# Reordering an expert loop: one branch for the first layer, its transposes behind the previous slot's second layer, gathers a slot sooner, the optional slots nested

## Chip, cores, metric

One core of one Trainium2 chip. The time is the device time of one execution in microseconds; several executions are taken and the median is quoted. TensorE (PE in the profile, PEld for its weight loads) does matrix products and transposes, ScalarE (ACT) and VectorE (DVE) the elementwise work, GpSimd (POOL) the gathers and scatters by index, and SyncE (SP) issues the plain transfers. Each engine runs its own instruction stream in order; streams wait for one another on semaphores. A name with a q behind it (PEldq, ACTq) is the sequencer of that engine: branches, waits, register loads.

## What is computed

A gated linear recurrence per head, then a dense layer of three maxed projections, then a mixture of eight experts in which each token goes to one expert. The change touches only the last part:

```python
logits = x @ w_gate                      # x: [3072, 384], 8 experts
e_idx = np.argmax(logits, axis=1)
gate_w = softmax(logits)[np.arange(N), e_idx]
eom = 1.0 / (1.0 + np.exp(-(x @ w_output_gate)))
for e in range(8):
    mask = e_idx == e
    h = np.maximum(x[mask] @ w1[e], 0.0)  # w1: [384, 1024]
    ye = h @ w2[e]                        # w2: [1024, 384]
    out[mask] = gate_w[mask, None] * eom[mask, e, None] * ye
```

## The kernel before

The tokens are sorted into slots of up to 128 tokens of one expert. There are 24 token tiles (NT) and so at most 32 slots (NS); how many are filled (`n_all`, from `meta`) depends on the data. Slots 0 to 2 (NF) belong to the largest expert and are begun while the routing of the last block of tokens is still computed. The loop over the other slots is unrolled, slots 24 to 31 behind a run-time condition `guard(j)`, `n_all > j`. In these inputs 30 slots are filled, 0 to 29.

A slot with at least 64 tokens, or one that is not the last of its expert, is *whole*: each of its products is three passes of rounded operands (hi times hi, hi times lo, lo times hi) with weights split beforehand by ScalarE (hi) and VectorE (lo). A last slot with fewer than 64 tokens is *alone* (`kind[j] == 1`): it is computed in plain fp32 straight from the staged weights, the two halves of the weights side by side. Which it is, is known at run time only, so each step holds both forms in an If/Else (`by_kind`).

The steps of slot j, in the names of the code:

- `gather(j)`: POOL fetches the slot's rows of x (384 values and the token's weight) into `xg[j]`, four buffers.
- `tx(j)`: 3 transposes of `xg` on PE into `psT`, then ACT (hi, L812, or plain, L816) and DVE (lo, L813).
- `cast1(j)`, `split2(j)`: if the expert is new (`new[j]`), 6 copies and 6 subtractions for the first layer's weights, 8 and 8 for the second's (L625, L626). Each layer has one buffer of split weights and two of staged ones (`stage`, SP, 1.5 MB each).
- `up(j, h)`: first layer, half h: 9 products of 512 columns (L844) and a copy to `hs` by ACT (L845). Alone: all of it in the call with h = 1 (L833, L853).
- `th(j)`: 8 transposes of `hs` (L884; alone 4, L889), then ACT's relu and DVE's remainder into `ch` (L863, L864; alone L890).
- `down(j)`: second layer, 24 products of 384 columns (L903; alone L833), then ACT scales with the token's weight (L917, `yo`; alone also L921 and L922) and POOL scatters to the output (L923).

The order on the engines is the order in which the code is written (a manual schedule). For slot j the loop writes: kinds of slot j+3 loaded into registers; 2 pieces of `split2(j)`; `gather(j+3)`; `up(j+1, 0)`; `th(j)`; the other 6 pieces of `split2(j)`; `up(j+1, 1)`; `tx(j+2)`; the first layer's weights of j+3 staged; `cast1(j+2)`; `down(j)`; the second layer's weights of j+2 staged.

Where a branch is not taken, the engines whose work it skips must still bring their semaphores to the count that the other way would have left. A form with work in both ways does that on its own instructions; a way that is empty on an engine gets an event instruction that waits until the engine has finished all it was given before, and then adds the count. `up(j+1, 0)` is such a case: written with `If(kind == 0)` and no Else.

Of the kernel before, what the change touches and what calls it, by code (L numbers as in the profile page):

```python
# [33 lines left out]
NS = NT + NE  # L34
# [54 lines left out]
def _layers(ctx, tc, pool_, wk, K, general, qk, al, a0, v, vT, w123, wout, gates, ew1, ew2, out):  # L89
# [508 lines left out]
    xg, cx, cxF, hs, ch, chg, new, eos, kind = ({} for _ in range(9))  # L598
# [105 lines left out]
    def slots_a_ops():  # L704
        ci = rtmp["ci"] = wt([128, NE], "ci", I32)
        nc.vector.scalar_tensor_tensor(ci, rtmp["ps"][:, 64:64 + NE], 127.0, gap, op0=ALU.add, op1=ALU.add)
        yield
        cj = wt([128, NE], "cj", I32)
        nc.vector.tensor_single_scalar(cj, ci, 7, op=ALU.arith_shift_right)
        yield  # L710
        nsl = wt([128, NE], "nsl")
        nc.vector.tensor_copy(nsl, cj)
        yield
        nf = wt([128, NE], "nf")
        nc.vector.tensor_mul(nf, nsl, nfirst)
        yield
        nc.vector.tensor_reduce(isf, nf, op=ALU.add, axis=AX.X)
        yield
        nc.vector.tensor_sub(nsl, nsl, nf)
        yield  # L720
        end = rtmp["end"] = wt([128, NE], "end")
        nc.vector.tensor_tensor_scan(end, one8, nsl, isf, ALU.mult, ALU.add)
        yield
        base = rtmp["base"] = wt([128, NE], "base")
        nc.vector.tensor_sub(base, end, nsl)
        yield
        bf = wt([128, NE], "bf")
        nc.vector.tensor_mul(bf, base, nfirst)
        yield
        nc.vector.tensor_sub(base, base, bf)  # L730
        yield
# [29 lines left out]
    def slots_e():  # L761

        end = rtmp["end"]
        rem = wt([128, NE], "rem", I32)
# [31 lines left out]

    def gather(j):
        xg[j] = C["cr"].tile([128, XW], F32, tag="xg", name="xg", bufs=4)
        n = TF * 128 if j < NF else NTOK
        nc.gpsimd.indirect_dma_start(out=xg[j], out_offset=None, in_=x2d[:n, :],  # L800
                                     in_offset=bass.IndirectOffsetOnAxis(ap=gidx[:, j:j + 1], axis=0),
                                     bounds_check=n - 1, oob_is_err=False)

    def tx(j):
        ps = bank(C["psT"], "T", "psT")
        for k in range(3):
            nc.tensor.transpose(ps[:, k * 128:(k + 1) * 128], xg[j][:, k * 128:(k + 1) * 128], ident)
        cx[j] = bp.tile([128, 2, DM], F32R, tag=("xH", "xL")[j % 2], name="cx")
        cxF[j] = bp.tile([128, DM], F32, tag="hH", name="cxF", bufs=7)
# [25 lines left out]
    def up(j, h):  # L835
        w1H, w1L = C["w1"]
        fs = slice(h * 512, h * 512 + 512)

        def whole():
            ps = bank(psM, "M", "psM1")  # L840
            for k in range(3):
                ks = slice(k * 128, (k + 1) * 128)
                for n, (x, w) in enumerate(((0, w1H), (0, w1L), (1, w1H))):
                    mm(ps, cx[j][:, x, ks], w[:, k, fs], start=(k + n == 0), stop=(k + n == 4))  # L844
            nc.scalar.copy(hs[j][:, fs], ps)  # L845

        def alone():
            ps = bank(psM, "M", "psM1")
            w = C["s1"][j % 2]
            for k in range(3):  # L850
                x = cxF[j][:, k * 128:k * 128 + 64]
                halves(ps, 512, (x, x), [w[:, k, g * 512:(g + 1) * 512] for g in range(2)], k == 0, k == 2)
            nc.scalar.copy(hs[j][:, :512], ps)  # L853

        if h == 0:
            hs[j] = bp.tile([128, FF2], F32, tag="x32", name="hs")
            with tc.If(kind[j] == 0) if j in kind else nullcontext():
                whole()
        else:
            by_kind(j, whole, alone)  # L860
# [14 lines left out]
    def th(j):  # L875
        ch[j] = bp.tile([128, 2, FF2], F32R, tag=f"o{j % 2}", name="ch", bufs=1)
# [17 lines left out]
    def down(j, fs=(0, NE)):  # L894
# [21 lines left out]
        gate = xg[j][:, DM:XW]  # L916
        nc.scalar.activation(y, ps[:, :DM], AF.Copy, scale=gate)  # L917
        if j in kind:
            with tc.If(kind[j] > 0):  # L919
                t = bp.tile([128, DM], F32, tag="hL", name="ylo", bufs=7)  # L920
                nc.scalar.copy(t[:64], ps[64:, :DM])  # L921
                nc.vector.scalar_tensor_tensor(y[:64], t[:64], gate[:64], y[:64], op0=ALU.mult, op1=ALU.add)  # L922
# [4 lines left out]
    def every():  # L927
        with tc.For_i(0, NTOK, 128) as r:
# [8 lines left out]
            for e in range(NE):  # L937
# [4 lines left out]
                for h in range(2):  # L942
                    up(0, h)
# [203 lines left out]
    then(up, 0, 0)  # L1147
    then(route_a, i)
    then(up, 0, 1)
    then(route_b, i)  # L1150
    then(th_whole, 0, 0)
    then(up, 1, 0)
# [4 lines left out]
    then(up, 1, 1)  # L1157
# [5 lines left out]
    then(up, 2, 0)  # L1163
    then(up, 2, 1)
# [35 lines left out]
    def guard(j):  # L1200
        return tc.If(n_all > j) if j >= NT else nullcontext()

# [10 lines left out]
    up(NF, 0)  # L1213
    up(NF, 1)
    tx(NF + 1)
    cast1(NF + 1)
    down(2)
    for j in range(NF, NS):
        if j + 3 < NS:
            load_meta(j + 3)  # L1220
            load_kind(j + 3)
        with tc.If(new[j] > 0):
            split2(j, range(2))
        if j + 3 < NS:
            gather(j + 3)
        with guard(j):  # L1226
            if j + 1 < NS:
                with guard(j + 1):
                    up(j + 1, 0)
            th(j)  # L1230
        with tc.If(new[j] > 0):
            split2(j, range(2, NE))
        if j + 1 < NS:
            with guard(j + 1):
                up(j + 1, 1)
                if j + 2 < NS:
                    tx(j + 2)
        if j + 3 < NS:
            stage(j + 3, ((0, "s1"),))
        if j + 2 < NS:  # L1240
            cast1(j + 2)
        with guard(j):  # L1242
            down(j)
        if j + 2 < NS:
            stage(j + 2, ((1, "s2"),))
# [50 lines left out]
```

## Time and profile before

| | us |
|---|---|
| median of 3 runs (754.25 to 758.59) | 754.65 |
| the profiled execution, its own time | 753.41 |
| its span, first to last instruction | 751.7 |
| PE busy in the span | 707.7 |
| DVE, ACT, POOL busy | 378.6, 305.8, 109.3 |

The span is what the profile shows; 1.7 us lie around it. The first filled slots begin at about 470 us, the loop over slots 3 to 29 at 494 us, and the last product ends at 740.7 us.

### The profile page before, as it was taken

What the parts mean: (1) busy time and instruction counts of PE and PEld (TensorE: products, weight loads), DVE (VectorE), ACT (ScalarE), POOL (GpSimd) and SP (SyncE); (2) the same over time, 40 slices, a digit from 0 to 9 for tenths busy, and PEclk for the clock granted to TensorE, in tenths of its full rate; (3) what the DMA queues carried; (4) which work ended last, traced back from release to release, by engine and by line L of the source; (5) the groups of instructions that cost most, each with busy time, mean ns of one, the idle gap of its engine ahead of it and who ended that gap; (6) DMA issues with size and microseconds to landing.
All of it is one profiled execution on the core that took longest, in us unless ns stands there. A gap on an engine that the chain in (4) does not pass through costs nothing. (4 is left out here: it accounts for less than half of the span.)

```text
span 751.7 us, 14582 instructions
## 1 busy us (share of the span) xinstructions
PE 707.7 (94%) x4750; PEld 627.8 (84%) x4750; DVE 378.6 (50%) x806; ACT 305.8 (41%) x750; POOL 109.3 (15%) x118
## 2 busy tenths in 40 slices
PE   7789999999999999999999999999999999999893
PEld 7668999888899998999999988899966789974663
DVE  7977887476976647546233366411115341111432
ACT  4355443554444434434222234333327453333552
POOL 1000000011120111111111130222222222222221
PEclk9999999999999999999999999999999999999997
DMA  9815400651510413100000050111387711179750
GB/s 259 349 39 157 145 1 22 183 135 28 143 40 22 129 44 106 38 22 10 16 24 13 21 200 33 49 39 44 128 303 285 280 45 44 54 263 392 284 211 17
DMA packets 23807, 86.78 MB, mean 115 GB/s; under 512 B 8004, under 2 KB 11868, under 8 KB 19600
## 3 DMA queue, kind: packets, MB, share of 16 engines
q1 hardware_dynamic: 18576, 73.54, 29.1%
q0 software_dynamic: 3968, 11.03, 4.5%
q10 hardware_dynamic: 1152, 0.89, 0.5%
q8 instruction: 51, 0.84, 0.5%
q14 instruction: 60, 0.49, 0.2%
HBM read 131.43 MB, written 10.63 MB: 189 GB/s over the span
## 5 line engine op out<-in xcount | busy, mean ns | idle before, releaser
L440 PE MATMUL hps<-xH,wH 128*128 128x384 f32 x432 | 104.0, 348 | 0.9 <-ACT xH L352 0.8
L903 PE MATMUL psP<-w2H,ch 128*128 128x384 f32 x368 | 101.4, 346 | 2.2 <-ACT ch L863 1.4
L466 POOL TENSOR_TENSOR hL<-hm,hH 128x384 fp32r<-128x384 f32 x36 | 42.2, 1172 | 399.9 <-ACT hH L461 399.8
L440 PE MATMUL hps<-xH,wL 128*128 128x384 f32 x432 | 98.4, 335 | 1.7 <-DVE wL L409 1.7
L440 PE MATMUL hps<-xL,wH 128*128 128x384 f32 x432 | 98.5, 335 | 0.0
L844 PE MATMUL psM<-w1H,cx 128*128 128x512 f32 x276 | 96.2, 404 | 0.8 <-ACTq L1204 0.8
L864 DVE SCALAR_TENSOR_TENSOR ch<-psH,ch 128x512 fp32r<-128x512 f32 x46 | 29.7, 686 | 106.1 <-ACT ch L863 105.8
L440 PEld LDWEIGHTS hps<-xH,wH 128*128 128x128 f32 x432 | 74.1, 188 | 6.9 <-ACT xH L352 1.5
L440 PEld LDWEIGHTS hps<-xH,wL 128*128 128x128 f32 x432 | 76.9, 188 | 2.3 <-DVE wL L409 2.3
L440 PEld LDWEIGHTS hps<-xL,wH 128*128 128x128 f32 x432 | 77.3, 188 | 0.2 <-DVE xL L353 0.2
L903 PEld LDWEIGHTS psP<-w2H,ch 128*128 128x128 f32 x368 | 68.1, 191 | 3.2 <-ACT ch L863 1.6
L476 PE MATMUL ops<-wo,hH 128*128 128x400 f32 x258 | 68.4, 346 | 0.4 <-ACT hH L461 0.3
L844 PEld LDWEIGHTS psM<-w1H,cx 128*128 128x128 f32 x276 | 51.9, 188 | 14.6 <-issue 1.8
L903 PE MATMUL psP<-w2L,ch 128*128 128x384 f32 x184 | 62.5, 340 | 0.0
L447 DVE TENSOR_TENSOR hm<-hm,hps 128x384 f32<-128x384 f32 x48 | 26.5, 551 | 69.6 <-PE hps L440 62.4
L923 POOL DMA_INDIRECT out<-yo,sidx x30 | 30.6, 1019 | 196.1 <-ACTq L919 132.9
L461 ACT CAST hH<-hm 128x384 fp32r<-128x384 f32 x43 | 22.0, 513 | 80.2 <-DVE hm L450 76.3
L844 PE MATMUL psM<-w1L,cx 128*128 128x512 f32 x138 | 54.5, 395 | 0.0
L917 ACT ACTIVATE yo<-psP,xg 128x384 f32<-128x384 f32 x30 | 17.4, 581 | 83.3 <-PE psP L903 64.1
L845 ACT COPY hs<-psM 128x512 f32<-128x512 f32 x46 | 27.0, 588 | 52.7 <-PE psM L844 48.2
L476 PEld LDWEIGHTS ops<-wo,hH 128*128 128x128 f32 x258 | 46.9, 188 | 1.5 <-ACT hH L461 0.7
L476 PE MATMUL ops<-wo,hL 128*128 128x400 f32 x129 | 44.4, 344 | 0.5 <-POOL hL L466 0.5
(215 smaller groups left out, 1145.7 us busy)
## 6 DMA issues: line engine op xcount, KB each, us to landing
s1a<-in_ew SPq DMA_DIRECT2D x15, 1536.0 KB
s2a<-in_ew SPq DMA_DIRECT2D x15, 1536.0 KB
s1b<-in_ew SPq DMA_DIRECT2D x15, 1536.0 KB
s2b<-in_ew SPq DMA_DIRECT2D x15, 1536.0 KB
ws<-in_w SPq DMA_DIRECT2D x6, 1152.0 KB
at<-in_al SPq DMA_DIRECT2D x16, 336.9 KB
vt<-in_v SPq DMA_DIRECT2D x8, 576.0 KB
x2d<-xs SPq DMA_DIRECT2D x24, 192.0 KB
```

The costliest lines, as they stand in the source:

```text
L440: mm(ps, slab(a, f)[:, w, k], b[i][:, k], start=(n == 0), stop=(n == 8))
L447: nc.vector.tensor_max(m, m, ps)
L461: nc.scalar.copy(hH[i, f], m)
L466: (nc.gpsimd if not general and i > 1 else nc.vector).tensor_sub(hL[i, f], hps["m"], hH[i, f].bitcast(F32))
L476: mm(ps[:, :DM + NG], a[i, f][:, ts_], wo[f // 3][:, b, f % 3], start=(f + n == 0), stop=(f + n == 7))
L844: mm(ps, cx[j][:, x, ks], w[:, k, fs], start=(k + n == 0), stop=(k + n == 4))
L845: nc.scalar.copy(hs[j][:, fs], ps)
L864: nc.vector.scalar_tensor_tensor(lo, ps, 0.0, hi.bitcast(F32), op0=ALU.max, op1=ALU.subtract)
L903: mm(ps[:, :DM], ch[j][:, x, f * 128:(f + 1) * 128], w[:, f], start=(f + n == 0), stop=(f == NE - 1 and n == 2))
L917: nc.scalar.activation(y, ps[:, :DM], AF.Copy, scale=gate)
L923: nc.gpsimd.indirect_dma_start(out=out[:, :], out_offset=bass.IndirectOffsetOnAxis(ap=sidx[:, j:j + 1], axis=0), in_=y, in_offset=None, bo ...
```

## The change

`up` loses its second call: one `by_kind` holds both halves (whole) or the alone form. `th(j+1)` is written behind `down(j)`. `tx` copies the token weight of `xg` into a small tile of its own (`gate`), so that `xg[j]` is free after `tx(j)` and no longer after `down(j)`, and `gather` runs four slots ahead in place of three. `split2(j)` is written in one piece. From slot 24 on each slot's work stands inside the condition of the one before it, and tiles made there are taken from an earlier slot (`held`). Some small tiles of the routing share a buffer under another name (left out below).

```diff
+    def held(tiles, j, n, make):
+        return tiles[j - n] if j >= NT + n else make()
+
     def gather(j):
-        xg[j] = C["cr"].tile([128, XW], F32, tag="xg", name="xg", bufs=4)
+        xg[j] = held(xg, j, 4, lambda: C["cr"].tile([128, XW], F32, tag="xg", name="xg", bufs=4))
...
     def tx(j):
+        gate[j] = held(gate, j, 4, lambda: wk.tile([128, 1], F32, tag="gate", name="gate", bufs=4))
+        nc.vector.tensor_copy(gate[j], xg[j][:, DM:XW])
         ps = bank(C["psT"], "T", "psT")
...
-    def up(j, h):
+    def up(j, hs_=(0, 1)):
         w1H, w1L = C["w1"]
-        fs = slice(h * 512, h * 512 + 512)
+        if hs_[0] == 0:
+            hs[j] = held(hs, j, 2, lambda: bp.tile([128, FF2], F32, tag="x32", name="hs"))
 
         def whole():
-            ps = bank(psM, "M", "psM1")
-            for k in range(3):
-                ks = slice(k * 128, (k + 1) * 128)
-                for n, (x, w) in enumerate(((0, w1H), (0, w1L), (1, w1H))):
-                    mm(ps, cx[j][:, x, ks], w[:, k, fs], start=(k + n == 0), stop=(k + n == 4))
-            nc.scalar.copy(hs[j][:, fs], ps)
+            for h in hs_:
+                fs = slice(h * 512, h * 512 + 512)
+                ps = bank(psM, "M", "psM1")
+                for k in range(3):
+                    ks = slice(k * 128, (k + 1) * 128)
+                    for n, (x, w) in enumerate(((0, w1H), (0, w1L), (1, w1H))):
+                        mm(ps, cx[j][:, x, ks], w[:, k, fs], start=(k + n == 0), stop=(k + n == 4))
+                nc.scalar.copy(hs[j][:, fs], ps)
...
-        if h == 0:
-            hs[j] = bp.tile([128, FF2], F32, tag="x32", name="hs")
-            with tc.If(kind[j] == 0) if j in kind else nullcontext():
-                whole()
-        else:
-            by_kind(j, whole, alone)
+        by_kind(j, whole, alone)
...
-        gate = xg[j][:, DM:XW]
-        nc.scalar.activation(y, ps[:, :DM], AF.Copy, scale=gate)
+        nc.scalar.activation(y, ps[:, :DM], AF.Copy, scale=gate[j])
...
-    up(NF, 0)
-    up(NF, 1)
+    up(NF)
     tx(NF + 1)
     cast1(NF + 1)
+    gather(NF + 3)
     down(2)
-    for j in range(NF, NS):
+    th(NF)
...
+    def turn(j):
         if j + 3 < NS:
             load_meta(j + 3)
             load_kind(j + 3)
+        if j + 4 < NS:
+            gather(j + 4)
         with tc.If(new[j] > 0):
-            split2(j, range(2))
-        if j + 3 < NS:
-            gather(j + 3)
-        with guard(j):
-            if j + 1 < NS:
-                with guard(j + 1):
-                    up(j + 1, 0)
-            th(j)
-        with tc.If(new[j] > 0):
-            split2(j, range(2, NE))
+            split2(j)
         if j + 1 < NS:
             with guard(j + 1):
-                up(j + 1, 1)
+                up(j + 1)
                 if j + 2 < NS:
                     tx(j + 2)
-        if j + 3 < NS:
-            stage(j + 3, ((0, "s1"),))
-        if j + 2 < NS:
-            cast1(j + 2)
-        with guard(j):
-            down(j)
-        if j + 2 < NS:
-            stage(j + 2, ((1, "s2"),))
+                    if j + 3 < NS:
+                        stage(j + 3, ((0, "s1"),))
+                    cast1(j + 2)
+        down(j)
+        if j + 1 < NS:
+            with guard(j + 1):
+                if j + 2 < NS:
+                    stage(j + 2, ((1, "s2"),))
+                th(j + 1)
+                if j + 1 >= NT:
+                    turn(j + 1)
+
+    for j in range(NF, NT):
+        turn(j)
```

## Rows read from the trace of the kernel before

**Rows 1.** Busy time by stretch: stretch, its length, busy us of each engine (instructions), TensorE clock, DMA.

```profile
552.00:608.00 56.00, 54.41 (x292) 38.12 (x293) 21.80 (x39) 30.59 (x63) 14.69 (x14) 1.00 0.74 266
608.00:670.00 62.00, 62.00 (x346) 56.39 (x343) 13.34 (x24) 20.80 (x41) 12.26 (x12) 1.00 0.27 86
670.00:741.00 71.00, 63.50 (x333) 43.05 (x331) 24.75 (x44) 34.65 (x70) 15.42 (x15) 0.98 0.71 264
```

**Rows 2.** Transposes of `hs`, 470 to 741 us, grouped (busy, mean ns | idle before <-releasers); PE's timeline.

```profile
L884 PE MATMUL psH<-ident,hs 128*128 128x128 f32 x160 | 20.9, 273 | 3.2 <-ACTq L919 1.5 <-PEq L857 1.1 <-PEq L1228 0.6
...
L889 PE MATMUL psH<-ident,hs 128*128 128x128 f32 x28 | 4.3, 275 | 2.3 <-ACT yo L917 0.9 <-ACTq L919 0.8 <-PEq L857 0.6
```

```profile
561.23 0.41 PE L889 MATMUL psH<-ident,hs 128*128 128x128 f32 x2 [0.59 <-PEq L857]
...
586.56 0.41 PE L884 MATMUL psH<-ident,hs 128*128 128x128 f32 x2 [0.56 <-PEq L857]
...
680.06 0.41 PE L889 MATMUL psH<-ident,hs 128*128 128x128 f32 x2 [0.84 <-ACTq L919]
```

**Rows 3.** Line 857 in the whole span: sequencer's duration ns min/median/max, first and last start.

```profile
L857 PEldq COMPARE_BRANCH  x50: 66/172/326, 481.8 to 722.5; - x50
...
L857 PEldq EVENT_SEMAPHORE  x7: 51/51/51, 551.5 to 714.3; - x7
```

**Rows 4.** ACT's timeline around 561 us.

```profile
560.67 0.58 ACT L917 ACTIVATE yo<-psP,xg 128x384 f32<-128x384 f32 x1 [3.64 <-PE psP L903]
```

**Rows 5.** PE's timeline, transposes of x and the second layer behind them, two slots.

```profile
581.57 0.41 PE L903 MATMUL psP<-w2H,ch 128*128 128x384 f32 x1 [0.30 <-PE psT L807]
...
708.88 0.52 PE L807 MATMUL psT<-ident,xg 128*128 128x128 f32 x3 [1.55 <-DMA xg<-x2d,gidx]
709.83 0.41 PE L903 MATMUL psP<-w2H,ch 128*128 128x384 f32 x1 [0.43 <-PE psT L807]
```

**Rows 6.** PE's timeline: the second layer of an alone slot.

```profile
564.99 2.80 PE L833 MATMUL psP<-s2a,hs 128*64 128x384 f32 x16
```

**Rows 7.** POOL's timeline, 698 to 701 us, and the gathers' time to landing, whole span.

```profile
698.39 1.00 POOL L923 DMA_INDIRECT out<-yo,sidx  x1 [6.73 <-ACT hs L845]
699.70 1.04 POOL L800 DMA_INDIRECT xg<-x2d,gidx  x1 [0.30 <-ACT hs L845]
```

```profile
DMA to landing us min/median/max: 3.0/4.0/9.1
```

**Rows 8.** Line 884 in one undisturbed slot, 502 to 506 us: first and last start.

```profile
L884 PE MATMUL psH<-ident,hs x6: 270/272/273, 505.4 to 506.0; 128*128 128x128 f32 x6
L884 PEldq EVENT_SEMAPHORE  x1: 51/51/51, 502.3 to 502.3; - x1
```

**Rows 9.** Line 787, registers for the kinds, on PE's sequencer.

```profile
L787 PEldq TENSOR_LOAD <-kinds x29: 297/302/483, 478.4 to 720.8; - x29
```

**Rows 10.** Line 685, a VectorE instruction of one element a partition.

```profile
L685 DVE TENSOR_SCALAR lack<-fm x1: 143/143/143, 435.1 to 435.1; 128x1 f32<-128x1 f32 x1
```

**Rows 11.** Slot 29, the last: timeline of PE, then of DVE.

```profile
731.86 1.06 PE L884 MATMUL psH<-ident,hs 128*128 128x128 f32 x8 [0.58 <-PEq L1228]
734.28 0.44 PE L903 MATMUL psP<-w2H,ch 128*128 128x384 f32 x1 [1.36 <-ACT ch L863]
...
735.01 0.98 PE L903 MATMUL psP<-w2H,ch 128*128 128x384 f32 x2
```

```profile
733.12 1.03 DVE L626 TENSOR_TENSOR w2L<-s2b,w2H 128x384 fp32r<-128x384 f32 x2
734.26 1.29 DVE L864 SCALAR_TENSOR_TENSOR ch<-psH,ch 128x512 fp32r<-128x512 f32 x2
```

**Rows 12.** Sequencers at the end: lines 1242, 80 and 1292.

```profile
L1242 POOLq INC_SWDGE_SEM  x2: 1382/1397/1412, 742.0 to 743.8; - x2
```

```profile
L80 PEldq COMPARE_BRANCH  x1: 4422/4422/4422, 742.7 to 742.7; - x1
```

```profile
L1292 POOLq DRAIN  x1: 5200/5200/5200, 745.7 to 745.7; - x1
```

More of the change, by code (lines that the diff above doesn't have):

```diff
@@ L597, in _layers @@
     C = {}
-    xg, cx, cxF, hs, ch, chg, new, eos, kind = ({} for _ in range(9))
+    xg, cx, cxF, hs, ch, chg, new, eos, kind, gate = ({} for _ in range(10))
     def open_right():
@@ L713, in slots_a_ops @@
         yield
-        nf = wt([128, NE], "nf")
+        nf = wt([128, NE], "fc")
         nc.vector.tensor_mul(nf, nsl, nfirst)
@@ L726, in slots_a_ops @@
         yield
-        bf = wt([128, NE], "bf")
+        bf = wt([128, NE], "fv")
         nc.vector.tensor_mul(bf, base, nfirst)
@@ L763, in slots_e @@
         end = rtmp["end"]
-        rem = wt([128, NE], "rem", I32)
+        rem = wt([128, NE], "cj", I32)
         nc.vector.tensor_single_scalar(rem, rtmp["ci"], 127, op=ALU.bitwise_and)
@@ L807, in tx @@
             nc.tensor.transpose(ps[:, k * 128:(k + 1) * 128], xg[j][:, k * 128:(k + 1) * 128], ident)
-        cx[j] = bp.tile([128, 2, DM], F32R, tag=("xH", "xL")[j % 2], name="cx")
-        cxF[j] = bp.tile([128, DM], F32, tag="hH", name="cxF", bufs=7)
+        cx[j] = held(cx, j, 2, lambda: bp.tile([128, 2, DM], F32R, tag=("xH", "xL")[j % 2], name="cx"))
+        cxF[j] = held(cxF, j, 2, lambda: bp.tile([128, DM], F32, tag="hH", name="cxF", bufs=7))
         def parts(hi, lo, p):
@@ L875, in th @@
     def th(j):
-        ch[j] = bp.tile([128, 2, FF2], F32R, tag=f"o{j % 2}", name="ch", bufs=1)
+        ch[j] = held(ch, j, 2, lambda: bp.tile([128, 2, FF2], F32R, tag=f"o{j % 2}", name="ch", bufs=1))
         p0 = bank(C["psH"], "H", "psH")
@@ L921, in down @@
                 nc.scalar.copy(t[:64], ps[64:, :DM])
-                nc.vector.scalar_tensor_tensor(y[:64], t[:64], gate[:64], y[:64], op0=ALU.mult, op1=ALU.add)
+                nc.vector.scalar_tensor_tensor(y[:64], t[:64], gate[j][:64], y[:64], op0=ALU.mult, op1=ALU.add)
         nc.gpsimd.indirect_dma_start(out=out[:, :], out_offset=bass.IndirectOffsetOnAxis(ap=sidx[:, j:j + 1], axis=0),
@@ L941, in every @@
                 split2(0)
-                for h in range(2):
-                    up(0, h)
+                up(0)
                 for h in range(2):
@@ L1146, in _layers @@
     i = NBLK - 1
-    then(up, 0, 0)
+    then(up, 0, (0,))
     then(route_a, i)
-    then(up, 0, 1)
+    then(up, 0, (1,))
     then(route_b, i)
     then(th_whole, 0, 0)
-    then(up, 1, 0)
+    then(up, 1, (0,))
     then(lambda: run(slots_a_ops(), route_c_ops(i), route_d_ops(i)))
@@ L1156, in _layers @@
     then(tx, 2)
-    then(up, 1, 1)
+    then(up, 1, (1,))
     then(slots_b)
@@ L1162, in _layers @@
     then(split_first, 2, NE - 1)
-    then(up, 2, 0)
-    then(up, 2, 1)
+    then(up, 2, (0,))
+    then(up, 2, (1,))
     then(slots_c)
@@ L1198, in _layers @@
         load_kind(j)
-    def guard(j):
-        return tc.If(n_all > j) if j >= NT else nullcontext()
     def cast1(j):
@@ L1212, in _layers, with guard @@
     cast1(NF)
-    up(NF, 0)
-    up(NF, 1)
+    up(NF)
     tx(NF + 1)
     cast1(NF + 1)
+    gather(NF + 3)
     down(2)
-    for j in range(NF, NS):
+    th(NF)
+    def guard(j):
+        return tc.If(n_all > j) if j >= NT else nullcontext()
+    def turn(j):
         if j + 3 < NS:
```

## The prediction

> **What bounds the kernel now.** I read the page first, for the shares: PE is busy for 707.7 of 751.7 us, so time can only be won where PE stands still, or by giving it less to do, and this change gives it the same products and transposes in another order. So the second view is the busy time by stretch, cut where the filled slots change their character [rows 1]. Between 608 and 670 us, where whole slots follow one another, PE is busy for 62.00 of 62.00 us: nothing to win there. Between 552 and 608 us 1.59 us are missing, between 670 and 741 us 7.50 us. In these two stretches lie the alone slots (10, 11, 14, 23, 24, 25, 28). DMA's share is 0.74 and 0.71 there against 0.27, since each of them needs weights of its own.
>
> The third view is the idle time ahead of the transposes of `hs`, first grouped, then one by one [rows 2]. The groups give 3.2 + 2.3 = 5.5 us in eight places; 0.58 us of it belong to the last slot [rows 11], and 4.9 us to seven places of 0.56 to 0.89 us, of which three rows stand. These are the transposes of the slots 9, 10, 13, 22, 23, 24 and 27, each the one before an alone slot; between two whole slots none are late. Twice the second layer begins late behind the transposes of x, by 0.30 and 0.43 us, and once these transposes wait 1.55 us for a gather [rows 5]: 2.28 us. The last slot has 0.58 and 1.36 us [rows 11]. Together 4.9 + 2.28 + 1.94 = 9.1 us, what is missing in the two stretches.
>
> **What causes the seven holes.** The view names several releasers for them, ACT's output step among them, and that has to be settled, because the answer decides on the sign of the change. In the old code the next slot's `up(j+1, 0)` is written ahead of these transposes, and for an alone slot its branch is empty on PE. The line's own rows show an event on PE's sequencer exactly seven times, from 551.5 to 714.3 us [rows 3], as many as there are alone slots, each at the end of the second layer before it. Such an event waits until PE is empty; behind it a branch (0.17 us [rows 3]), a wait and the first weight load have to run with nothing queued. The rival cause is ACT's output step `yo`, which ends at about the same time. But at 561.23 us PE starts while `yo` runs until 560.67 + 0.58 = 561.25 us [rows 4]: here at least it isn't waited for. I take the emptied queue as the cause of all seven; from slot 23 on, as at 680.06 us, a guard comes on top (0.84 against 0.56 and 0.59 us [rows 2]).
>
> **The change, part by part.**
>
> *One branch for the first layer.* Neither form is empty on PE any more, so the seven events go: −4.9 us at most. What is late next? `th(j+1)` now stands behind `down(j)` and needs ACT's copy of `hs(j+1)`. ACT makes it right behind `split2(j)`, which `down(j)` itself needs, and `down(j)` then runs for 2.8 us even where it is alone [rows 6]; so the copy is there. In return ACT's relu of `th(j+1)` has all of `up(j+2)` to end in, in place of one half. Nothing new is late on PE, and I take the full 4.9 us. The reordering itself costs nothing: the same 53 PE instructions of a whole slot, with one changeover fewer.
>
> *The path of the sequencer.* Between `th(j+1)` and `up(j+2)` PE's sequencer now loads the next kind (0.30 us [rows 9]) and passes some three branches of 0.17 us [rows 3], about 1.05 us with the checks. Before, this stood behind `down`. Is there work in the queue to hide it? The wait ahead of the transposes of one slot is passed at 502.3 us, and these start at 505.4 us [rows 8]: the sequencer is 3.1 us ahead. So 1.05 us are hidden. If only the eight transposes covered it (0.9 us, as they start 0.11 us apart [rows 8]), 0.15 us would show in each of 26 slots, 4 us. I take 0 and keep 4 as a bound. [...]
>
> *Gathers a slot sooner.* The gather of slot 28 is issued at 699.70 us, right behind the scatter that POOL takes first [rows 7], and lands just before its transposes start at 708.88 us, about 9 us later. The slowest of the run took 9.1 us, the median 4.0 us [rows 7]. The two late second layers (0.30, 0.43 us) are of the same origin: where PE's sequencer is held at a gather until just before the transposes, it isn't ahead any longer, and the branches behind them show. In the new order the gather keeps its place behind the scatter of slot j−1 but is the one of slot j+4: it gets one more slot, at least two stretches of 2.8 us [rows 6], one for each layer. −2.28 us. On POOL it is the same number of instructions. Its buffer is free since `tx(j)`, two slots back, so it waits for nothing new, and nor does the scatter behind it.
>
> *The copy of the weight.* One VectorE instruction of one element a partition per slot, 0.14 us by the nearest row [rows 10], 30 times, on a VectorE that is busy for 13.34 of 62 us where whole slots follow one another [rows 1]; it waits for the gather as PE's transposes do, and VectorE's next step waits for these anyhow. 0 us.
>
> *`split2` in one piece.* For a new expert's slot its first two pieces now come behind ACT's relu instead of ahead of it. Where `up(j+1)` lies between, that is covered. The last slot has no `up` behind it. In the old order two pieces precede the relu, and PE's products start at 734.28, and in earnest at 735.01 us, with VectorE's remainder for `ch` [rows 11]. In the new order the relu comes about 0.9 us sooner, but the second product needs VectorE's first w2L, behind 1.29 us for `ch`: 734.26 − 0.9 + 1.29 + 0.5 = 735.15 us [rows 11]. From there on both run at the same pace; the clock, 1.00 elsewhere and 0.98 over the last stretch [rows 1], I leave as it was. I put the last slot at +0.1 us, between −0.6 (its hole of 0.58 us counts after all) and +0.6 (one more piece is waited for).
>
> *Nesting.* Filled slots from 24 on pass two guards where there were four; hidden as above. Behind the last slot, POOL passes the empty slots 30 and 31: two count instructions of 1.4 us and branches, then 5.2 us until it is empty [rows 12], which is the end of the program. Nested, the two counts stay, since two scatters are skipped, some branches go, and six levels have to be left. I take 0, between −1.5 (one count for both) and +2.
>
> *Staging.* Its order on SP is the old one; the alone slots come up to 0.9 us sooner, and their weights are issued a full slot or more ahead. 0 us.
>
> **The sum.** 4.9 + 2.28 − 0.1 = 7.1 us. On the profiled execution: 753.41 − 7.1 = 746.3 us. The median of the runs stands 1.24 us above that execution, so 747.5 us, 0.95% less. A measurement of this kernel tells about 1% from no change, so this forecast lies on the line.
>
> **Rivals.**
>
> *A. The sequencer shows* (0.15): 4 us come back at the start of `up`, 751.5 us. For it: the holes of 0.30 and 0.43 us are of that kind [rows 5]. Against it: the 3.1 us [rows 8].
>
> *B. Transposes wait for `yo`* (0.07), the slower side: if the transposes do need ACT's output step, then, as they stand right behind `down(j)` in every slot now, 27 slots pay 4.9 / 7 = 0.7 us each, 18.9 us, less the 7.1 us won: 766.5 us. From 7.1 / 0.7 = 10 slots on the change loses. For it: the groups put 3.2 of 5.5 us down to ACT [rows 2]. Against it: the overlap at 561.23 us [rows 2, 4].
>
> *C. The gather isn't sooner* (0.08): it stays behind the scatter on POOL, and if its buffer comes free late, only 4.8 us are won: 749.8 us. Against it: the buffer's last reader moves ahead by two steps.
>
> *D. The end shrinks too* (0.12): one count instruction and the branches go, 1.4 us or more, 746.1 us or less.
>
> *E. A far jump* (0.06): the skip over slots 30 and 31 is one long jump now. The longest jump of the program, over the code of line 80, holds PE's sequencer for 4.42 us [rows 12], against 0.17 us for a usual branch; on POOL it would add some 3 to 4 us to the end: 751 us. [...]
>
> **How the numbers follow.** The forecast has 0.52, by itself 746 to 749 us. The range, 745.0 to 752.5 us, takes in A, C, E and most of D; B is left out. Faster by over 1% (below 747.1 us): a good third of the forecast's own, and D, 0.33. Slower by over 1%: B and a little, 0.08. Within 1%: 0.59.
>
> **What the new profile would show.** Right: no event of PE's sequencer in `up`; the first transposes of the slots before the alone ones without idle time; those of slot 28 without a wait for DMA; PE full from 552 to about 733 us but for the last slot. Wrong: idle time of PE ahead of `th` with ACT as its releaser in whole slots (B), or ahead of `up` with PE's sequencer (A); a longer stretch from the last scatter to the end (E).

## The result, and the profile after

The changed kernel takes 748.40 us in the median of 22 runs (742.36 to 754.86), the kernel before 755.71 us in as many runs beside it (749.95 to 759.73): a ratio of 0.9898, 95% interval 0.9874 to 0.9922. Forecast were 747.5 us and a range of 745.0 to 752.5 us. The profiled execution took 750.23 us with a span of 748.4 us, only 3.3 us less than the one of before; so the first thing to settle is where these two traces part.

They part long before the change. Busy time by stretch of the kernel after, and behind it the same ten microseconds of the kernel before (columns as in [rows 1]):

```profile
40.00:50.00 10.00, 8.93 (x63) 7.61 (x64) 5.61 (x11) 5.38 (x16) 0.00 (x0) 0.50 0.01 2
```

```profile
40.00:50.00 10.00, 8.33 (x90) 6.81 (x91) 7.43 (x13) 6.31 (x18) 0.00 (x0) 1.00 0.02 5
```

In this execution TensorE's granted clock was 0.83 from 30 to 40 us, 0.50 from 40 to 50 us and 0.65 from 50 to 60 us, in work that the change doesn't touch, where the kernel before has 1.00 in all three; and all that follows stands about 5.6 us later: the first transposes of x behind slot 2's first layer begin at 487.07 us, not at 481.44. (In two kernels of the experiments below, whose clock from 30 to 60 us was 0.66 and 1.00, they begin at 488.03 and 481.70 us.) In both kernels the long executions are mostly those with the lower mean clock (in the changed one 0.976 at 754.86 us, 0.996 at 742.36 us; in the one before, beside the experiments, 0.976 at 760.83 us, 0.995 at 750.22 us); where in an execution the clock falls, only the one profiled shows. I therefore compare from there on. Call S the stretch from these transposes (slot 3's) to the end of the last work that isn't slot 29's second layer. First the kernel before, then after, over S:

```profile
481.44:732.92 251.48, 242.89 (x1320) 194.17 (x1320) 66.20 (x114) 103.77 (x205) 55.61 (x54) 1.00 0.50 179
```

```profile
487.07:730.82 243.75, 241.46 (x1320) 194.67 (x1320) 69.91 (x141) 104.12 (x203) 55.47 (x54) 1.00 0.51 184
```

The same 1320 PE instructions take 7.73 us less: PE's idle time falls from 8.59 to 2.29 us, its busy time by 1.43 us. The last slot's second layer with its waits takes 8.23 us against 7.75, the end behind the last product 9.39 against 11.03. So −7.73 + 0.48 − 1.64 = −8.89 us, and with the 5.63 us of the early clock −3.3 us, the difference of the spans. In this one pair of executions the change is worth −8.89 us. The medians of many runs say −7.3 us, the ratio about −7.7; why less, no run shows.

Where is the idle time left? The stretches that answer to [rows 1], 5.6 us later, and PE's groups from 486 to 741 us (as in [rows 2]):

```profile
557.60:613.60 56.00, 56.00 (x306) 40.56 (x305) 25.52 (x51) 32.77 (x67) 14.49 (x14) 1.00 0.74 271
613.60:675.60 62.00, 62.00 (x346) 55.21 (x346) 12.55 (x25) 21.01 (x39) 13.75 (x14) 1.00 0.29 96
675.60:730.80 55.20, 53.68 (x293) 35.85 (x289) 18.97 (x39) 28.13 (x56) 11.88 (x12) 1.00 0.86 321
```

```profile
L907 PE MATMUL psP<-w2H,ch 128*128 128x384 f32 x345 | 94.6, 345 | 1.7 <-ACT w2H L625 1.7
L853 PE MATMUL psM<-w1H,cx 128*128 128x512 f32 x240 | 80.6, 404 | 2.0 <-ACT w1H L625 1.3 <-ACTq L1203 0.8
L907 PE MATMUL psP<-w2L,ch 128*128 128x384 f32 x173 | 58.9, 340 | 0.5 <-DVE w2L L626 0.5
...
L888 PE MATMUL psH<-ident,hs 128*128 128x128 f32 x160 | 21.0, 274 | 0.0
...
L893 PE MATMUL psH<-ident,hs 128*128 128x128 f32 x28 | 4.4, 278 | 0.0
```

Ahead of the transposes of `hs` (L888, L893) PE now stands idle for 0.0 us, where [rows 2] have 3.2 and 2.3; the stretch around slots 9 to 14 is full. Of the group L853, 0.8 us are the wait at slot 3, which both kernels have; the 1.3 us behind ACT's `w1H` are new. The timelines of PE, then of ACT, then of SP show where they come from:

```profile
694.11 0.66 PE L893 MATMUL psH<-ident,hs 128*128 128x128 f32 x4
696.02 0.49 PE L853 MATMUL psM<-w1H,cx 128*128 128x512 f32 x1 [1.25 <-ACT w1H L625]
696.74 0.50 PE L853 MATMUL psM<-w1L,cx 128*128 128x512 f32 x1 [0.23 <-DVE w1L L626]
```

```profile
695.35 3.23 ACT L625 CAST w1H<-s1a 128x512 fp32r<-128x512 f32 x6 [3.37 <-DMA s1a<-in_ew]
```

```profile
681.32 0.33 SPq L794 DMA_DIRECT2D s2a<-in_ew  x1
684.51 0.33 SPq L794 DMA_DIRECT2D s1a<-in_ew  x1
687.73 0.33 SPq L794 DMA_DIRECT2D s2b<-in_ew  x1
```

Slot 26 opens a new expert. Its first layer waits 1.48 us for the cast weights, ACT for the transfer: issued at 684.51 us, used from 695.35 us, nearly 11 us. The DMA engines (last columns: share and GB/s) are full all that time (1.01), behind a stretch in which they were not (0.61):

```profile
664.00:676.00 12.00, 12.00 (x67) 9.41 (x65) 2.73 (x5) 4.31 (x8) 3.92 (x4) 1.00 0.61 208
676.00:700.00 24.00, 22.48 (x120) 13.08 (x117) 5.63 (x12) 10.34 (x20) 4.25 (x5) 1.00 1.01 402
```

At the end, slot 29 in PE's timeline, and the sequencers of PE and POOL at line 1240, to be set beside [rows 11, 12]:

```profile
729.73 1.09 PE L888 MATMUL psH<-ident,hs 128*128 128x128 f32 x8
732.56 0.44 PE L907 MATMUL psP<-w2H,ch 128*128 128x384 f32 x1 [1.74 <-ACT w2H L625]
733.47 0.69 PE L907 MATMUL psP<-w2L,ch 128*128 128x384 f32 x1 [0.46 <-DVE w2L L626]
```

```profile
L1240 PEldq COMPARE_BRANCH  x2: 184/850/1517, 737.0 to 739.2; - x2
...
L1240 POOLq COMPARE_BRANCH  x2: 38/44/50, 739.8 to 741.5; - x2
...
L1240 POOLq INC_SWDGE_SEM  x1: 1427/1427/1427, 740.0 to 740.0; - x1
```

The last slot's waits are 2.20 us, against 0.58 + 1.36 + 0.11 = 2.05 us before. POOL counts once (INC_SWDGE_SEM), not twice.

### The profile page after: what moved, and what is told of

Same layout as the page of the kernel before. It is cut to its first block, busy times and chain, and to the rows that moved or that the text cites. A ratio compares the mean times of both kernels' runs of the same rounds, so it can differ in the third digit from the quotient of the medians.

```text
span 748.4 us, 14138 instructions
## 1 busy us (share of the span) xinstructions
PE 714.6 (95%) x4750; PEld 635.8 (85%) x4750; DVE 381.7 (51%) x837; ACT 306.8 (41%) x750; POOL 109.8 (15%) x118
## 3 DMA queue, kind: packets, MB, share of 16 engines
q0 software_dynamic: 3968, 11.03, 4.5%
## 5 line engine op out<-in xcount | busy, mean ns | idle before, releaser
L853 PE MATMUL psM<-w1H,cx 128*128 128x512 f32 x276 | 92.9, 404 | 2.0 <-ACT w1H L625 1.3
L853 PEld LDWEIGHTS psM<-w1H,cx 128*128 128x128 f32 x276 | 52.0, 188 | 13.9 <-ACT w1H L625 1.5
L853 PE MATMUL psM<-w1L,cx 128*128 128x512 f32 x138 | 54.7, 396 | 0.2 <-DVE w1L L626 0.2
L920 ACT ACTIVATE yo<-psP,gate 128x384 f32<-128x384 f32 x30 | 17.4, 581 | 82.9 <-PE psP L907 67.9
```

What stands on the lines that cost most here:

```text
L920: nc.scalar.activation(y, ps[:, :DM], AF.Copy, scale=gate[j])
```

## The experiments

Each ratio is to the kernel before, run beside it, with medians of 753.57 to 756.11 us; so ratios compare across rows better than medians do. S, PE's idle time in it and the end (from the last product to the end of the span) are those of one profiled execution each. Three more kernels, which leave part of the weights out, stand behind the table; two of them have one execution.

| kernel | S, us | idle in S | of it gathers / holes at the empty branch / slot 26 | end, us | median, us (95% interval of the ratio) |
|---|---|---|---|---|---|
| before | 251.48 | 8.59 | 2.28 / 4.96 / 0 | 11.03 | 755.71 (1) |
| after | 243.75 | 2.29 | 0 / 0 / 1.48 | 9.39 | 748.40 (0.9874 to 0.9922) |
| before, gathers sooner | 248.55 | 6.09 | 0 / 4.75 / 0 | 11.00 | 752.56 (0.9956 to 1.0023) |
| before, one branch | 249.17 | 5.96 | 5.20 / 0 / 0 | 11.04 | 750.76 (0.9917 to 0.9983) |
| after, two branches | 245.25 | 3.85 | 0 / 3.05 / 0 | 9.39 | 746.84 (0.9868 to 0.9945) |
| after, gathers later | 248.78 | 5.32 | 4.56 / 0 / 0 | 9.88 | 751.39 (0.9924 to 0.9999) |
| after, not nested | 244.70 | 2.97 | 0 / 0 / 1.47 | 11.01 | 749.56 (0.9896 to 0.9960) |
| after, second weights later | 267.45 | 16.72 | 0 / 0 / 0 | 9.39 | 773.13 (1.0184 to 1.0274) |
| after, four pieces early | 243.86 | 2.01 | 0 / 0 / 1.00 | 9.60 | 746.97 (0.9864 to 0.9949) |
| after, three buffers | 241.63 | 0.77 | 0 / 0 / 0 | 9.39 | 743.84 (0.9829 to 0.9922) |

**The gathers alone.**

```diff
...
-        if j + 3 < NS:
-            gather(j + 3)
+        if j + 4 < NS:
+            gather(j + 4)
```

> The kernel before, with nothing but the gather of slot j+4 in place of slot j+3 and the copy of the weight column that this needs. Measured by the stretch from the first transpose of slot 3's x to the end of the last product, which no early stretch disturbs: 259.2 us in the kernel before, 252.0 us in the changed one. My theory: the 2.28 us of late gathers (1.55 us ahead of the transposes of x, 0.43 and 0.30 us ahead of two second layers) go, the seven holes ahead of the transposes of hs stay: 257.0 us, and the time behind the last product stays at 11.0 us. The device time falls by 2.3 us, 0.3%. Rival C (the gather isn't sooner): 259.2 us.

The edit has the copy of the token weight too (left out above). The gather waits are gone and the holes at the branch are there, as PE's groups show:

```profile
L887 PE MATMUL psH<-ident,hs 128*128 128x128 f32 x160 | 20.9, 273 | 3.2 <-ACTq L921 1.4 <-PEq L1231 0.6 <-PEq L860 0.6
L810 PE MATMUL psT<-ident,xg 128*128 128x128 f32 x84 | 14.1, 277 | 0.8 <-issue 0.8
```

To the last product it is 256.25 us where 257.0 was expected; over S −2.93 us, of which 2.50 are idle time. Rival C falls: the gather is sooner. The device time moves less than its interval.

**One branch alone.**

```diff
-            if j + 1 < NS:
-                with guard(j + 1):
-                    up(j + 1, 0)
             th(j)
...
-                up(j + 1, 1)
+                up(j + 1)
```

> The kernel before, with nothing but the first layer of slot j+1 in one branch, behind the transposes of slot j's hs, so that these stand behind the second layer of slot j-1 in every slot. Gathers, the guards and the two pieces of split2 are the old ones. Theory of the empty branch: the seven holes (4.9 us) go and the late gathers (2.28 us) stay, while slot 26 may wait up to 1.5 us for its first layer's weights, as it does in the changed kernel: the stretch from slot 3's transposes of x to the last product falls from 259.2 to between 254.3 and 255.8 us. Rival B (the transposes wait for ACT's output step): 0.7 us of idle time ahead of them in each of 27 slots, 259.2 - 4.9 + 18.9 = 273 us.

Half right. No hole is left ahead of the transposes of `hs` (27 slots have them right behind a second layer here, and rival B's 0.7 us is in none), but to the last product it is 257.33 us, above the expected range: the gathers' waits grew from 2.28 to 5.20 us.

```profile
L882 PE MATMUL psH<-ident,hs 128*128 128x128 f32 x160 | 20.9, 274 | 0.0
L807 PE MATMUL psT<-ident,xg 128*128 128x128 f32 x84 | 14.1, 277 | 4.9 <-DMA xg<-x2d,gidx 4.0 <-issue 0.9
```

The holes had hidden these waits. The gather whose transposes stand at 571.08 us here is issued at the old time (560.34 us; S begins 6.59 us later, so 553.75 on the old clock, against 553.68). But PE comes to these transposes 1.5 us sooner, and the gather takes 10.6 us to land in place of 8.7; before, it was 2.1 us in time.

**Two branches at the new place.** The undo of the same part:

```diff
-            for h in hs_:
+            for h in (hs_[:1] if j in kind else hs_):
...
+        if j in kind:
+            with tc.If(kind[j] == 0):
+                whole()
+            hs_ = (1,)
         by_kind(j, whole, alone)
```

> The changed kernel, with the first layer of slot j in two branches again (the first half if the slot is whole; then the second half or the whole of the alone form), both at the new place. Theory of the empty branch: seven events of PE's sequencer are back in the line of the first layer, at the same slots, each with a hole of 0.56 to 0.89 us, which now stands ahead of the alone form's first products instead of ahead of the transposes of hs, since the place of the empty branch makes it, not the work behind it. The three holes of the slots 23 to 25 may be paid by the 1.5 us that slot 26 waits for its weights, which then go: the stretch of 252.0 us becomes 255.4 to 256.9 us. Rival: the holes came from where the transposes of hs stood (ACT's output step, or its copy of hs): no holes, 252.0 us.

The seven events are back, now in line 865, the new first condition; and the holes stand ahead of the alone form's first products:

```profile
L865 PEldq EVENT_SEMAPHORE  x7: 51/51/51, 552.8 to 710.2; - x7
```

```profile
553.18 1.08 PE L839 MATMUL psM<-s1a,cxF 128*64 128x512 f32 x4 [0.42 <-PEq L865]
```

Six of 0.42 and one of 0.53 us, 3.05 us in all; slot 26 no longer waits; S is 1.50 us longer, as 3.05 − 1.48 says. So the cause stands, and the hole goes where the empty branch goes, but its size was expected too high (0.56 to 0.89). To the last product it is 252.18 us, below the expected 255.4 to 256.9, for two reasons: the holes are smaller, and the last slot's second layer, with a granted clock of 1.00 in the ten microseconds around it and not 0.83, took 6.93 us, not 8.23. That stretch is no measure for a difference of 1 us; S is a better one. By the device time, one can't tell this kernel from the changed one (ratios 0.9906 and 0.9898).

**The gathers later again.**

```diff
-        if j + 4 < NS:
-            gather(j + 4)
+        if j + 3 < NS:
+            gather(j + 3)
```

> The changed kernel, with the gathers of slot j+3 again, all else as it is. Theory: a gather that is issued a slot later lands just before its transposes or behind them, as in the kernel before: about 2.3 us of idle time ahead of the transposes of x of slot 28 and of two second layers; the stretch of 252.0 us becomes 254.3 us. If only the wait of slot 28 counts: 253.5 us. Rival: the new order alone makes the old distance enough, since the gather now stands ahead of the whole first layer: 252.0 us.

More than expected: 4.56 us of waits in seven places, two of them for slot 28:

```profile
707.11 0.52 PE L813 MATMUL psT<-ident,xg 128*128 128x128 f32 x3 [1.73 <-DMA xg<-x2d,gidx]
708.17 0.66 PE L907 MATMUL psP<-w2H,ch 128*128 128x384 f32 x1 [0.55 <-PE psT L813]
```

S is 5.03 us longer: +4.56, −1.48 as slot 26's weights are in time again, and 2 us of busy time at a clock of 0.96 behind 690 us. The rival falls. Of the 4.56 us, 2.67 stand where the kernel before has its 2.28 (ahead of slot 28 and of an earlier second layer); the other 1.89 us, in two slots where it has none, are there because PE, without the holes, comes sooner.

**Not nested.** Each guard for itself, `with guard(j)` around `down(j)` and so on; the order stays. Staging and casts (`stage`, `cast1`) stand outside the guards again, as before.

> The changed kernel, with the guards of the slots from 24 on side by side as they were before, not nested; order, gathers and the one branch stay. Theory: the nesting is what shortened the end: the two skipped scatters of the slots 30 and 31 are counted twice again, and the time from the last product to the end of the program goes from 9.35 back to 11.0 us, while the stretch from slot 3 to the last product stays at 252.0 us within 0.3 us: device time +1.7 us. Rival 1: the end is shorter because the last transfers of weights no longer stand behind the last slot, or by chance: 9.35 us stays. Rival 2: the two extra guards of each slot from 24 on are seen on PE as well: the stretch grows by 0.2 us or more in each of six slots, 253 us.

The end is 11.01 us again, with two counts of 1.4 us:

```profile
L1239 POOLq INC_SWDGE_SEM  x2: 1392/1402/1412, 735.5 to 737.3; - x2
```

So the nesting gives the 1.6 us, most of it by the count of 1.4 us. Rival 1 isn't tested apart: the edit also brings back a staging issue of SP behind the last slot (0.07 us at 734.30 us). The second count, on POOL's way to the end, accounts for the time without it. S is 0.95 us longer, more than the 0.3 expected, but not by guards: 0.57 us are a wait of slot 24's second layer for its weights and 0.16 us a wait for a cast; 0.27 us are busy time. A kernel without this edit (the next one) has the first of them too, 0.54 us.

**A transfer cut, the wrong one.**

```diff
-            nc.sync.dma_start(out=C[s][j % 2], in_=...
+            m = 1 if (n, j) == (1, 26) else (3, NE)[n]
+            nc.sync.dma_start(out=C[s][j % 2][:, :m], in_=...[:, :m],
```

> The changed kernel, but of the second layer's weights of slot 26 only an eighth is loaded (the rest of that tile keeps the weights of slot 24, so the outputs of this slot's expert are others). In the changed kernel the weights for slot 26's first layer are issued at 684.5 us, and ACT can begin with them at 695.4 us; PE waits 1.25 + 0.23 us. The second layer's weights, issued 3.2 us later, are not needed before 706 us. Theory (the transfers share the DMA engines, and a later one slows an earlier one): without 1.4 MB at 0.41 MB per us the first layer's weights are there up to 3.4 us sooner, the 1.48 us go, and the stretch of 252.0 us becomes 250.5 us. Rival (transfers are served in the order of their issue): what is issued later changes nothing, 252.0 us, and the wait stays.

The wait stayed, 1.23 + 0.23 us, which would be the rival's sign; but the expectation had taken slot 25's transfer for slot 26's. The latter is issued 1 us before slot 26's first-layer weights are used, so this run tells nothing of the cause, and the next two cut others.

**A transfer ahead of it cut, and one behind it.** The same edit with (1, 24), then with (1, 25).

> The run with an eighth of slot 26's second-layer weights cut the wrong transfer: in the changed kernel those are issued at 694.36 us, 1 us before the first-layer weights of slot 26 are taken, and could not have slowed them. The transfers that could are slot 24's second-layer weights (issued 681.32 us, ahead of slot 26's first-layer weights at 684.51 us) and slot 25's (687.73 us). Here the changed kernel loads only an eighth of slot 24's second-layer weights (this slot's expert then computes with the rest of the old ones). Theory (the DMA engines are full from 676 to 700 us, and a transfer waits for those issued ahead of it): 1.4 MB less ahead of it at 0.41 MB per us, slot 26's weights come 3.4 us sooner, and PE's wait of 1.25 + 0.23 us is gone: from slot 3's transposes of x to the last slot's second layer 243.75 us becomes 242.3 us. Rival (the casts, not the transfer, are late; or another transfer counts): the wait stays, 243.75 us.

> The counterpart to the cut of slot 24's transfer, which took PE's wait away: here the changed kernel loads only an eighth of slot 25's second-layer weights (this slot's expert then computes with the rest of the old ones). They are issued 3.2 us behind slot 26's first-layer weights (687.73 against 684.51 us) and 7.6 us before these are there. If transfers are served in the order of their issue, what comes behind takes nothing from them: PE's wait of 1.25 + 0.23 us ahead of slot 26's first layer stays, 243.75 us from slot 3's transposes of x to the last slot's second layer. If all transfers under way share the DMA engines evenly, slot 26's weights had at most half of them from 687.73 us on and come 2 us or more sooner: the wait is gone, 242.3 us.

Each of the two is one execution. With slot 24's transfer cut, ACT starts the cast at 686.26 us; S begins 6.43 us earlier here than in the kernel after, so that is 692.69 us on its clock, 2.66 us sooner (3.4 expected), and PE waits no more: S 241.64 us, against 242.3 expected. With slot 25's cut, nothing changes: the cast waits until 695.50 us (S begins 0.14 us earlier), PE waits 1.23 + 0.23 us, S is 244.02 us (0.32 us of it a wait of slot 24's second layer). ACT's timeline of the one, then of the other:

```profile
686.26 3.22 ACT L625 CAST w1H<-s1a 128x512 fp32r<-128x512 f32 x6 [0.68 <-DMA s1a<-in_ew]
```

```profile
695.50 3.22 ACT L625 CAST w1H<-s1a 128x512 fp32r<-128x512 f32 x6 [3.63 <-DMA s1a<-in_ew]
```

So with an eighth of the transfer issued 3.2 us ahead of them, slot 26's first-layer weights are used 2.66 us sooner; with an eighth of the one issued behind them, no sooner (695.64 us on the clock of the kernel after, against 695.35). Service in the order of issue would give that; beyond these two transfers no run shows it.

**Second-layer weights behind the first's.**

```diff
                     cast1(j + 2)
+                if j > NF + 1:
+                    stage(j + 1, ((1, "s2"),))
```

> The changed kernel, with the second layer's weights of slot j+1 issued by SP behind the first layer's weights of slot j+3, in place of ahead of them: for slot 26 this is at about 698 us in place of 687.7 us; nothing is left out. Theory of shared DMA engines: the first layer's weights of slot 26 are there by 692 us, PE's wait of 1.48 us goes, and the second layer's weights still land before ACT and DVE take them (706 us): the stretch of 252.0 us becomes 250.5 us. Rival 1 (served in the order of issue): 252.0 us, nothing changes ahead of slot 26. Rival 2: held back, the second layer's weights are themselves late in the alone slots 23 to 25, which read them straight: waits of 1 to 3 us ahead of their second layers, 253 to 258 us.

Rival 2, and worse than priced (277.68 us to the last product, against 253 to 258): five waits of 3.6 to 4.6 us, the first in slot 10, the last in slot 29, behind S:

```profile
571.48 0.99 PE L839 MATMUL psP<-s2a,hs 128*64 128x384 f32 x4 [4.62 <-DMA s2a<-in_ew]
```

SP's place behind slot j+3's weights isn't reached before slot j+1's first layer is done (in the kernel after, slot 24's ends at 684.33 us, and slot 26's weights are issued at 684.51 us), and the transfer then takes longer than what is left, by these 3.6 to 4.6 us. The idle time is not all of the price: S is 23.70 us longer than in the changed kernel, 14.43 us by idle and 9.27 us by busy time for the same 1320 products and transposes, at a mean clock of 0.96 against 1.00:

```profile
484.79:752.24 267.45, 250.73 (x1320) 200.30 (x1320) 69.99 (x141) 104.61 (x203) 55.32 (x54) 0.96 0.47 165
```

**Four pieces ahead of the output step.**

```diff
+        def ahead():
+            with guard(j + 1):
+                with tc.If(new[j + 1] > 0):
+                    split2(j + 1, range(4))
...
-        down(j)
+        down(j, before=ahead if j + 1 < NS else None)
```

> The changed kernel, with the first four of the eight pieces of split2 of slot j+1 written ahead of ACT's output step of slot j, thus ahead of the relus of slot j+1; the other four where they were. It is meant for the last slot, whose second layer waits 1.74 us for ACT's w2H and 0.46 us for DVE's w2L. Theory: four pieces are ready when the relu is, and the wait falls to some 0.4 us: the stretch of 252.0 us becomes 250.2 us; if PE keeps the higher clock for the last products (0.83 on the mean over 730 to 740 us now), 1 to 2 us more. Rival: the pieces wait for the second layer of slot j and hold ACT's output step and the relus of each new expert's slot; these then are late for the second layer: new holes behind the first layers, 252 us or more.

The theory falls: the last slot waits 2.93 us instead of 2.20. ACT's timeline says why, then PE's:

```profile
725.56 1.75 ACT L625 CAST w2H<-s2b 128x384 fp32r<-128x384 f32 x4 [2.55 <-DMA s2b<-in_ew]
727.22 0.57 ACT L922 ACTIVATE yo<-psP,gate 128x384 f32<-128x384 f32 x1
```

```profile
728.96 0.69 PE L907 MATMUL psP<-w2H,ch 128*128 128x384 f32 x1 [2.93 <-ACT ch L867]
```

Slot 29's second-layer weights aren't there before 725.56 us, 0.6 us after PE has begun the transposes; ACT stood still for 2.55 us with the output step and the relus queued behind. The rival had named this queue, with another wait at its head.

**Three buffers for the first layer's weights.** The third one takes two planes of new space and the one-hot rows of the routing, which are dead by then.

```diff
-        C["s1"] = [cr.tile([128, 3, FF2], F32, name="s1a"), None]
+        C["s1"] = [cr.tile([128, 3, FF2], F32, name="s1a"), None, None]
...
+        C["s1"][2] = cl.tile([128, 2, FF2], F32, name="s1c")
...
-                    if j + 3 < NS:
-                        stage(j + 3, ((0, "s1"),))
+                    if j + 4 < NS:
+                        stage(j + 4, ((0, "s1"),))
```

> The changed kernel with three buffers for the first layer's raw weights in place of two, and their transfer issued one slot sooner (slot j+4's behind the first layer of slot j+1); nothing is left out. Theory (the depth of the staging makes PE wait in slot 26: with two buffers the DMA engines stand half idle from 664 to 676 us and are full from then to 700 us, with three the transfer of slot 26's first-layer weights is issued at 676.7 us in place of 684.5 us): the wait of 1.25 + 0.23 us ahead of slot 26's first layer is gone, and from slot 3's transposes of x to the last slot's second layer 243.75 us becomes 242.3 us; device time 1.5 us less than the changed kernel's. Rival 1 (what the first layer's weights gain, the second layer's lose: one more transfer is ahead of slot 24's second-layer weights, which now come just in time for 691.4 us): a wait of 1 to 3 us moves to the second layers of the slots 24 and 25, 243.5 to 246 us. Rival 2 (the wait is not one for the transfer): 243.75 us.

As the theory had it, and a little more. Its S, and PE's group of the first layer in it:

```profile
482.49:724.12 241.63, 240.86 (x1320) 194.41 (x1320) 69.81 (x141) 104.22 (x203) 56.05 (x54) 1.00 0.52 186
```

```profile
L864 PE MATMUL psM<-w1H,cx 128*128 128x512 f32 x240 | 80.6, 403 | 0.8 <-ACTq L1214 0.8
```

PE is idle for 0.77 us in S, all of it at slot 3. No wait moved to the second layers, so rival 1 falls. Over S it is 2.12 us less than in the changed kernel, 1.52 of them idle time. The median, 743.84 us, is 4.6 us below the changed kernel's, but the kernel before beside it was 2.1 us faster too (753.57 against 755.71); the ratio is 0.9876 against 0.9898. Its interval (0.9829 to 0.9922) lies below 1 and overlaps with that of the changed kernel: by the trace it is better than both kernels, by the device time only than the one before.

## Why the prediction was right, and where two errors met

**Seven holes, −4.9 us: right.** They sum to 4.96 us and are gone. That the empty branch makes them, not the place of the transposes or ACT's output step, the two runs on the branch show from both sides; rival B's wait is nowhere, with the transposes behind every second layer.

**Gathers, −2.28 us: right in size, wrong as a term of its own.** Alone the step takes 2.50 us of idle time away. The branch alone takes 5.54 us of holes away, the last slot's among them, and gives 2.92 us back in gather waits. Over S that is −2.93 and −2.31 us; with both steps and the nesting it is −7.73. Taken out of the changed kernel the gathers are worth 4.56 us. The prediction added two terms of which each hid part of the other's wait; it came out right since both were made. With the branch alone, the same sum would have missed by 2.9 us. And the median of 4.0 us [rows 7] hid two cases: in the kernel before, the gathers issued between 608 and 660 us land after 3.2 to 3.9 us, those between 672 and 708 us, where the DMA share is 0.70 to 1.01 in steps of ten microseconds, after 6.5 to 9.1 us.

**Sequencer, copy of the weight: 0, right.** Between the transposes and the first layer there is no hole in any slot from 4 on but 26, so the 3.1 us of lead [rows 8] did cover the 1.05 us, and rival A falls.

**Last slot, +0.1 us: right by its waits** (2.05 to 2.20 us, +0.15). The second product was forecast for 735.15 us in old times; with the 7.73 − 0.58 = 7.15 us won ahead of it that is 728.0 us, and it starts at 733.47 − 5.63 = 727.84 us.

**Staging, 0 us: wrong.** "Their weights are issued a full slot or more ahead" held for the issue, not for the landing. [Rows 1] had shown a DMA share of 0.71 over 71 us; that mean hid 30 us with the engines all but full, 0.94 from 670 to 680 us, 0.94 from 690 to 700 us, and between them 1.01, as this row of the kernel before shows:

```profile
680.00:690.00 10.00, 9.05 (x49) 4.05 (x51) 0.61 (x1) 3.22 (x6) 2.72 (x3) 1.00 1.01 415
```

In the changed kernel the share is 1.01 over 24 us. The three alone slots 23 to 25 need new weights each, and PE now takes them faster than the transfers come in: +1.48 us, nearly a third of the 4.96 given back, as the cut transfer and the third buffer show.

**Nesting and the end, 0 us: wrong, −1.64.** It is rival D (0.12), count for count: one count of 1.4 us goes, with some branches [rows 12]. Rival E's long jump exists, on PE: 1.52 us in line 1240 against 0.17 us for a usual one, while its last products still run, and on POOL, where it would have hurt, the branch takes at most 0.05 us. That POOL's branch would take as long as PE's was the author's estimate; why PE's does, no run shows.

**Busy time, no term: −1.68 us** (S −1.43, last slot −0.25), for the same instructions. The kernels with few holes have mostly the lower sums (240.86 us with one, 241.46 with three, 242.89 with twelve). In part that is how a hole is counted: the last product ahead of one counts with its whole 0.34 us, where without a hole the next starts 0.18 us on, as in these two ahead of the hole at 561.23 us [rows 2]:

```profile
560.12 0.34 PE L903 MATMUL psP<-w2L,ch 128*128 128x384 f32 x1
560.30 0.34 PE L903 MATMUL psP<-w2H,ch 128*128 128x384 f32 x1
```

For nine holes fewer that is 9 times 0.16 = 1.4 us, an estimate. It doesn't fit every kernel: with two branches there are eight holes, ahead of other products, and 241.40 us. How much of the 1.68 us this explains stays open.

In sum, for the two traces: −4.96 − 2.28 + 0.15 + 1.48 − 1.64 − 1.68 = −8.93 us, against −7.1 forecast. The two missed steps, +1.48 and −1.64, cancelled: that was luck. And as the medians moved by −7.3 us, 1.6 us less than these traces, that 748.40 us came so near to 747.5 us says nothing for the single terms; the waits in the traces do.

## What to carry to other kernels

Waits in series hid each other here (without the holes, gather waits of 2.28 us became 5.20 us): when one is taken away, look up for each following one by how much it was in time, and cost edits together, not one by one. For staged transfers ask when they land, from the bytes queued ahead in the densest stretch, not when they are issued or what the mean share is. An `If` with nothing in it for PE wasn't free in these kernels: each time it emptied PE's queue, for 0.42 to 0.89 us.

## What the hardware showed beyond that

The end of a wait for a transfer came behind most of the traffic: with four pieces early, the DMA share is 0.59 in 723 to 724 us and 0.05 in 724 to 725 us, and the wait for that transfer ends at 725.56 us. The share is a mean of 16 engines; which of them came last it doesn't say. And the clock at the end isn't set by the last slot's wait alone: with the same 1.74 + 0.46 us the granted clock of the ten microseconds around it was 0.83 in the kernel after and 1.00 in the one with two branches, where this second layer took 1.3 us less (6.93 us against 8.23); why, no run shows.
